# Attention and a two-layer feed-forward: weight signs carried by Prelu, inverse sums applied after the value product, q split by a difference

## The chip, the cores and the metric

The kernel runs on one core of one Trainium2 chip. The core's engines work side by side, each on its own instruction queue: TensorE (PE) multiplies matrices into PSUM; VectorE (DVE), ScalarE (ACT) and GpSimd (POOL) do elementwise work; SyncE (SP) issues DMAs. POOL does not read PSUM in this kernel. The metric is the time of one execution on the device in microseconds (us), lower is better.

## The reference

Eight batches of eight heads, 576 tokens, head dimension 64. Attention is causal by blocks of 64 tokens. Its output, heads side by side, is 4608 tokens of width 512 and goes through two layers with a leaky ReLU between them. q and k are about normal with a spread of 0.58, v of 0.1.

```
scores = q @ k.T / sqrt(64)
scores = where(pos_i // 64 >= pos_j // 64, scores, -1e9)
attn = exp(scores - max) ; attn = attn / (sum(attn) + 1e-9)
x = attn @ v                      # (4608, 512) after the heads are joined
h = x @ w_in                      # w_in (512, 2048), handed over in float64
out = maximum(0.01 * h, h) @ w_out  # w_out (2048, 512), float64
```

q, k and v are float32 and the weights are float64 in memory. The output is float32.

## The kernel before

**Precision and tiling.** A token row of scores needs up to 576 keys; each head has five query tiles (t = 0 to 4, the first of 64 tokens, the others of 128; tile t sees 64(2t+1) keys). Most products are made in pairs of 16-bit or rounded parts (a high part and the low part that is left), which keeps float32-like precision: q and k in `float32r` parts (`qs`, `kk`), v, x, the weights and the hidden layer in float16 parts. A matmul on full float32 data takes two PE records, and the trace shows each at about twice the time per column of a float32r or float16 one.

**Kinds of work.** Batch 0 is done as 8 `lo` items (tokens 0 to 319) and 8 `hi` items (320 to 575), with full float32 matmuls and no splitting (but for the scores of the `hi` items of heads 6 and 7, which are split as below): scores (L561), probabilities `p` in `prow` (the exponential, L609, whose row sums go to `sums`), inverse sums `rec` (L624 to L628, with a factor 2^15), `p` multiplied by `rec` in place (`normalising`, L676 to L678, on POOL, DVE or ACT), `p` transposed by PE (L724) and copied out of PSUM to `ptf` (`copying`, L259 and L260), value products into 64 rows of the PSUM bank `p_t` (L769), and a copy into `xr` (`put_x`, L748, through L259 or L260). Batch 1 is done as `first` items (tokens 0 to 191) and `rest` items (the others), batches 2 to 7 as whole heads (`full`, 48 of them). These split `p` into float16 parts (L653 to L658), transpose them by a DMA, and make value products with float16 operands (L784).

**The q and k split** (L521 to L534) of `first`, `rest` and `full`: q and k each stand twice, on partitions 0 to 63 and 64 to 127. `qs` gets 0.125 q rounded (L262 on ACT or L263 on DVE), then its lower half is replaced by the rest, 0.125 q minus the rounded part (L529, DVE only). `kk[:,0]` gets k rounded (L259 or L260), `kk[:,1]` the rest of k on all 128 partitions (L269 on DVE or L270 on POOL). One float32r matmul with each half of `kk` (L572) sums the high and low part of q over the 128 partitions.

**Weights.** Thirty-two pieces (16 of w_in, 16 of w_out), each 128 x 512 values of 8 bytes. A load goes to one of three buffers `raw` (L407). A piece takes four steps: the upper 32-bit word, read as float32, is scaled by 2^-112 (L411 ACT, L412 POOL or L413 DVE); the byte below the upper word gives further mantissa bits (L415, ACT); the sign bit of the upper word is merged into that (L416, DVE); the scaled word is shifted left by 3 bits, which drops its own sign, and joined with the result (L420, DVE). Then PE takes a Gram matmul of the piece (L434) for the size of the weights; after a layer's last piece follow the common scale and the split of all 16 pieces into float16 parts (L467 to L472).

**Feed-forward.** Eighteen chunks of 256 tokens: x is scaled and split (L905 to L909), the first layer (L925) writes `p_h`, ACT applies the leaky ReLU as Prelu (L930), a cast and a difference make the parts `gh` and `gl` (L259 or L260, L269 or L270) in a ring of 8, and the second layer (L943) sums in `p_o`.

**What sets the order.** Every instruction is handed to `Plan` with its candidate engines, an estimated cost, a rank, and what it reads and writes. `Plan.run` places them by a list schedule: an engine takes the ready operation with the lowest rank, and a second candidate is offered `HOLD` ns later than the first. The result is the fixed order of each engine's queue. Ranks count heads (batch 0's items count 1 each) and come from the constants at the top: `OFF1`, `SL1`, `AHEAD` and `OFF2` place the weight pieces, their loads and their splits, `RL` and `VD` the loads of q, k and v, `RP`, `RB`, `RN`, `RT`, `RV` and `RX` the steps of a head, `LEAD`, `LAG`, `RS` and `RG` the feed-forward. While PE would stand idle early on, the plan puts in a filler matmul of the identity (L1009), whose result is not used; it keeps PE at work.

Of the kernel before, what the change touches and what calls it, by code (L numbers as in the profile page):

```python
# [9 lines left out]
F32 = mybir.dt.float32  # L10
# [27 lines left out]
RW = -0.059  # L38

RL = 2.33  # L40
RP = 0.343
RB = 0.475
RT = 2.736
RV = 2.331
RX = -3.93
RN = -0.627

LEAD = 3.395
LAG = 1.993
RS = 2.118  # L50
RG = -0.005
OFF1 = 2.95
OFF2 = -5.023
SL1 = 10.227
AHEAD = 0.756

LAT = 1550
HOLD = 236.003
# [4 lines left out]
LOAD = 108  # L63
RATE = 0.4414
# [10 lines left out]
STEPA = 0.555  # L75
STEPB = 0.884
VD = 2.806
# [165 lines left out]
def attention_ffn(ctx: ExitStack, tc: tile.TileContext, qk0: bass.AP, qk: bass.AP, v: bass.AP, w_in: bass.AP, w_out: bass.AP, out: bass.AP):  # L243
# [13 lines left out]
    def copying(n, dst, src, sb=True, by=None, first="ACT", fast=True):  # L257
        if by is None:
            one = lambda: nc.scalar.copy(dst(), src())  # L259
            two = lambda: nc.vector.tensor_copy(dst(), src())  # L260
        else:
            one = lambda: nc.scalar.activation(dst(), src(), AF.Copy, scale=by)  # L262
            two = lambda: nc.vector.tensor_scalar_mul(dst(), src(), by)  # L263
        both = [("ACT", act(n, sb), one), ("DVE+" if sb and fast else "DVE", dve(n, sb and fast), two)]
# [18 lines left out]
    make_identity(nc, ident)  # L283
    ones = fixed([P, P], F32, "ones")
# [25 lines left out]
    for y in range(2):  # L310
        nc.gpsimd.memset(sums[y], 1.0)
# [65 lines left out]
    def weight_piece(num, rank, f, out_side):  # L377
# [26 lines left out]
        if src.dtype != F32:  # L404

            def load():
# [3 lines left out]
            add([  # L410
                ("ACT", act(w, True) + 70, lambda: nc.scalar.activation(val(), top(), AF.Copy, scale=2.0**-112)),  # L411
                ("POOL", pool1(w), lambda: nc.gpsimd.tensor_scalar(val(), top(), 2.0**-112, 1.0, op0=ALU.mult, op1=ALU.mult)),  # L412
                ("DVE+", dve(w), lambda: nc.vector.tensor_scalar_mul(val(), top(), 2.0**-112)),  # L413
            ], rank, [t_key], [v_key])
            add([("ACT", act(w, True) + 70, lambda: nc.scalar.activation(word(0), byte(), AF.Copy, bias=-15.5 / 32, scale=1 / 32))], rank, [], [r_key])  # L415
            add([("DVE+", dve(w) + 45, lambda: nc.vector.scalar_tensor_tensor(  # L416
                word(0), word(1), -2147483648, word(0), op0=ALU.bitwise_and, op1=ALU.bitwise_or
            ))], rank, [t_key], [r_key])
# [57 lines left out]
    def attention(i):  # L476
# [7 lines left out]
        plain_s, plain_v = kind == "lo" or kind == "hi" and h < HS, kind in ("lo", "hi")  # L484
# [39 lines left out]
        else:  # L524
            qd, khd, kld = qs[z][:, qa:qe], kk[z][:, 0, :ke], kk[z][:, 1, :ke]
            add(copying(qe - qa, lambda: qd, lambda: q_in, by=scale), rp, [qkey], [("qs", z)])
            add(copying(ke, lambda: khd, lambda: k_in), rp, [qkey], [("kh", z)])
            add(
                [("DVE+", dve(qe - qa) + 120, lambda: nc.vector.scalar_tensor_tensor(  # L529
# [517 lines left out]
```

## Time and profile before

| | |
|---|---|
| median of 3 runs | 1092.83 us (1090.83 to 1092.85) |
| the profiled execution | 1092.42 us |
| its span, first to last instruction | 1090.6 us |
| mean granted TensorE clock | 0.994 |
| busy: PE, DVE, ACT, POOL | 1047.4, 696.3, 671.3, 373.8 us |

A row of a group reads: line, engine, operation, out<-in by the program's names, out<-in as partitions x elements and type, xcount, then busy us and mean ns of one, then the engine's idle time before them and what ended it. A row of a stretch of the span gives each engine's busy us with its instruction count, then the granted clock, the DMA share and GB/s. A row in order of time gives start, duration, engine, line and operation. A row of waits gives who waited, for whom, the total in us, how many times, and the longest. PEld is PE's loading of the stationary operand, which overlaps PE.

### The profile page before, as it was taken

How to read it: one execution, taken by the hardware profiler on the slowest of the kernel's cores; microseconds unless marked ns; L12 is line 12 of the kernel's file. 1: busy time of each engine (PE TensorE's matmuls, PEld its weight loads, DVE VectorE, ACT ScalarE, POOL GpSimd, SP SyncE). 2: the span in 40 equal slices, each digit the busy share in tenths (PEclk: the TensorE clock that was granted, in tenths of full speed). 3: DMA queues.
4: the chain of work that ended last, by engine and by line, in shares of the span. 5: the costliest groups of instructions: out<-in, count | busy, mean ns of one | idle time of the engine just before them, and what ended most of it. 6: DMA issues, size and time to landing. Idle time of an engine off the chain costs nothing. (4 is left out here: it accounts for less than half of the span.)

```text
span 1090.6 us, 21865 instructions
## 1 busy us (share of the span) xinstructions
PE 1047.4 (96%) x8282; PEld 761.6 (70%) x8282; DVE 696.3 (64%) x1698; ACT 671.3 (62%) x1611; POOL 373.8 (34%) x423
## 2 busy tenths in 40 slices
PE   9999889999998889999999999999999999999998
PEld 7877557677665666677777777777777777766665
DVE  6797867888887787875655667777777775100000
ACT  5788846877787677655655575666666655322222
POOL 1112224445555443433323334333334342211221
PEclk9999999999999899999999999999999999999999
DMA  7837334798978577847355355757575654000000
GB/s 272 269 124 237 91 90 113 149 214 177 183 152 183 103 162 146 177 99 158 82 125 104 88 128 116 157 112 153 121 155 121 125 82 95 1 20 11 10 20 20
DMA packets 251017, 134.85 MB, mean 124 GB/s; under 512 B 221728, under 2 KB 232992, under 8 KB 250912
## 3 DMA queue, kind: packets, MB, share of 16 engines
q1 hardware_dynamic: 250912, 133.46, 53.0%
q8 instruction: 65, 1.06, 0.4%
q14 instruction: 40, 0.33, 0.1%
HBM read 68.94 MB, written 9.44 MB: 72 GB/s over the span
## 5 line engine op out<-in xcount | busy, mean ns | idle before, releaser
L925 PEld LDWEIGHTS <-wih 128*128 128x128 f16 x2304 | 222.3, 99 | 72.2 <-issue 3.2
L270 POOL TENSOR_TENSOR gl<-g,gh 128x512 bf16<-128x512 f32 x115 | 136.5, 1188 | 284.3 <-ACT gh L259 246.0
L925 PE MATMUL p_h<-slab,wih 128*128 128x256 f16 x1152 | 197.9, 274 | 3.2 <-DVE xi L896 2.2
L930 ACT ACTIVATE g<-p_h 128x512 f32<-128x512 f32 x144 | 85.0, 591 | 154.5 <-PE p_h L925 149.5
L943 PE MATMUL p_o<-woh,gh 128*128 128x512 f16 x576 | 172.2, 381 | 0.0
L943 PE MATMUL p_o<-woh,gl 128*128 128x512 f16 x576 | 172.1, 380 | 0.0
L943 PE MATMUL p_o<-wol,gh 128*128 128x512 f16 x576 | 171.9, 380 | 0.0
L943 PEld LDWEIGHTS <-gh 128*128 128x128 f16 x1152 | 107.2, 99 | 80.7 <-issue 1.3
L592 DVE TENSOR_REDUCE nm<-p_s 128x1 f32<-128x320 f32 (+4 forms) x308 | 140.8, 488 | 31.6 <-ACT prow L609 15.1
L925 PE MATMUL p_h<-xh,wih 128*128 128x256 f16 x576 | 158.2, 275 | 0.3 <-ACT g L930 0.3
L925 PE MATMUL p_h<-xl,wih 128*128 128x256 f16 x576 | 158.0, 274 | 0.0
L925 PE MATMUL p_h<-xh,wil 128*128 128x256 f16 x576 | 157.9, 274 | 0.0
L925 PE MATMUL p_h<-slab,wil 128*128 128x256 f16 x576 | 157.8, 274 | 0.0
L572 PE MATMUL p_s<-kk,qs 128*128 128x288 f32 (+3 forms) x592 | 124.3, 334 | 24.6 <-ACT slab L609 15.2
L609 ACT ACTIVATE prow<-p_s,nm 128x448 f32<-128x448 f32 (+4 forms) x168 | 88.4, 530 | 75.7 <-DVE nm L592 71.1
L925 PEld LDWEIGHTS <-wil 128*128 128x128 f16 x1152 | 113.4, 98 | 14.9 <-issue 1.2
L572 PEld LDWEIGHTS p_s<-kk,qs 128*128 128x128 f32 x592 | 90.9, 190 | 45.5 <-ACT slab L609 22.8
L609 ACT ACTIVATE slab<-p_s,nm 128x320 f32<-128x320 f32 (+4 forms) x140 | 72.5, 522 | 63.4 <-DVE nm L592 62.6
L270 POOL TENSOR_TENSOR kk<-qk_in,kk 128x576 fp32r<-128x576 f32 (+1 forms) x51 | 75.6, 1483 | 89.2 <-ACT kk L259 34.4
L943 PEld LDWEIGHTS <-gl 128*128 128x128 bf16 x576 | 56.5, 98 | 68.4 <-issue 0.8
L658 DVE SCALAR_TENSOR_TENSOR slab<-prow,rec,slab 128x320 f16<-128x320 f32 (+4 forms) x140 | 85.9, 648 | 22.5 <-ACT slab L654 20.1
L784 PEld LDWEIGHTS <-vs 128*128 128x128 f16 x1680 | 85.9, 98 | 11.1 <-issue 2.5
(135 smaller groups left out, 1524.0 us busy)
## 6 DMA issues: line engine op xcount, KB each, us to landing
qk_in<-in_qk SPq DMA_DIRECT2D x56, 576.0 KB, 4.3
raw<-in_w_in SPq DMA_DIRECT2D x16, 512.0 KB, 4.7
raw<-in_w_out SPq DMA_DIRECT2D x16, 512.0 KB, 4.5
out<-ob SPq DMA_DIRECT2D x18, 256.0 KB, 2.4
out<-slab SPq DMA_DIRECT2D x18, 256.0 KB, 3.1
v_raw<-in_v SPq DMA_DIRECT2D x7, 640.0 KB, 6.2
raw<-in_v SPq DMA_DIRECT2D x7, 640.0 KB, 5.7
qk_in<-in_qk SPq DMA_DIRECT2D x8, 416.0 KB, 3.7
```

The costliest lines, as they stand in the source:

```text
L270: ("POOL", pool2(n) - (0.25 * n if n == 512 else 0), lambda: nc.gpsimd.tensor_sub(dst(), one(), two())),
L572: go = lambda ap=ap, cols=cols, c=c, k0=k0, k1=k1, first=first, last=last: nc.tensor.matmul(ap, qs[z][:, cols], kk[z][:, c, k0:k1], start= ...
L592: [("DVE", dve(kw[t]), lambda t=t, ap=ap, flat=flat: nc.vector.tensor_reduce(nm[z][: qn[t], t : t + 1], ap[: qn[t]], axis=AX.X if flat els ...
L609: nc.scalar.activation(o, ap[: qn[t]], AF.Exp, bias=nm[z][: qn[t], t : t + 1], scale=scale / 2 if plain_s else 1.0, accum_out=sums[z][: qn ...
L658: ("DVE+", dve(w) + 62, lambda: nc.vector.scalar_tensor_tensor(part(1), p, by, part(0), op0=ALU.mult, op1=ALU.subtract)),
L784: nc.tensor.matmul(p_t[x][:, c : c + src.free_size()], vs[z][:, (j + 1) % NT], src, start=start, stop=stop)
L925: nc.tensor.matmul(hh[:, i, :], w[:, f, d, :], x[:, d, :], start=k == 0, stop=k == len(terms) - 1)
L930: add([("ACT", act(512), lambda: nc.scalar.activation(g[z], hh, AF.Prelu, alpha=0.01, scale=DOWN))], rank, [("h", z)], [("g", z)])
L943: nc.tensor.matmul(p_o[m], a[:, i, m * P : (m + 1) * P], w[:, 2 * u + i, :], start=u == 0 and k == 0, stop=u == NU - 1 and k == 5,)
```

## The change

Five things change.

- **Weight pieces.** The upper word is scaled by a Prelu on ACT with slope 2^32 for negative values, so a negative value's exponent is 32 higher. After the left shift by 3, this exponent bit is the sign bit. The merge of the sign (L416) is gone, and so are the POOL and DVE forms of the scaling (L412, L413).
- **Batch 0.** `normalising` is gone; `p` stays unnormalised. A float32 matmul per tile of `rec`, spread over 64 columns, with the identity puts the inverse sums of all tokens on 64 partitions of the other PSUM bank (`spread`). The copy into `xr` now copies these, and a DVE multiplication by the value product follows, in place.
- **The q and k split.** Both copies take a factor per partition from a new constant `eighth`: q is scaled by 0.125 on partitions 0 to 63 and by 1 on the others, k the other way round. q's low part is then a plain difference on 64 partitions, on DVE or POOL; k's low part is only made on partitions 0 to 63, with zeros on the others from the start. The copy's ACT form is planned with 93 ns more.
- **`first` items** take the full float32 scores of batch 0 (`plain_s`), with no split of q and k.
- **Constants.** The ranks and engine offers are refitted, and the plan now knows a longer load (`LOADS`, 190 ns) for the score matmuls, 108 before.

```
-RL = 2.33
+RL = 4.147
-RP = 0.343
+RP = -0.26
-RT = 2.736
+RT = 3.569
-RX = -3.93
+RX = -5.745
-RN = -0.627
+RN = -1.226
-LEAD = 3.395
+LEAD = 3.858
-OFF1 = 2.95
-OFF2 = -5.023
-SL1 = 10.227
-AHEAD = 0.756
+OFF1 = 3.4
+OFF2 = -3.708
+SL1 = 12.623
+AHEAD = -3.272
-STEPB = 0.884
-VD = 2.806
+STEPB = 0.691
+VD = 1.444
...
+    eighth = fixed([P, 2], F32, "eighth")
+    nc.gpsimd.memset(eighth, 1.0)
+    nc.gpsimd.memset(eighth[0:64, 0:1], scale)
+    nc.gpsimd.memset(eighth[64:128, 1:2], scale)
...
+        nc.gpsimd.memset(kk[y][64:128, 1].bitcast(F32), 0.0)
...
-            add([
-                ("ACT", act(w, True) + 70, lambda: nc.scalar.activation(val(), top(), AF.Copy, scale=2.0**-112)),
-                ("POOL", pool1(w), lambda: nc.gpsimd.tensor_scalar(val(), top(), 2.0**-112, 1.0, op0=ALU.mult, op1=ALU.mult)),
-                ("DVE+", dve(w), lambda: nc.vector.tensor_scalar_mul(val(), top(), 2.0**-112)),
-            ], rank, [t_key], [v_key])
+            add([("ACT", act(w, True) + 70, lambda: nc.scalar.activation(val(), top(), AF.Prelu, alpha=2.0**32, scale=2.0**-112))], rank, [t_key], [v_key])
...
-            add([("DVE+", dve(w) + 45, lambda: nc.vector.scalar_tensor_tensor(
-                word(0), word(1), -2147483648, word(0), op0=ALU.bitwise_and, op1=ALU.bitwise_or
-            ))], rank, [t_key], [r_key])
...
-        plain_s, plain_v = kind == "lo" or kind == "hi" and h < HS, kind in ("lo", "hi")
+        plain_s, plain_v = kind == "lo" or kind == "hi" and h < HS or kind == "first", kind in ("lo", "hi")
...
+            add(copying(qe - qa, lambda: qd, lambda: q_in, by=eighth[:, 0:1]), rp, [qkey], [("qs", z)])
+            add(copying(ke, lambda: khd, lambda: k_in, by=eighth[:, 1:2]), rp, [qkey], [("kh", z)])
+            add(subtracting(qe - qa, lambda: qd[64:128], lambda: q_in[64:128], lambda: qd[64:128]), rp, [qkey], [("qs", z)])
+            add(subtracting(ke, lambda: kld[0:64], lambda: k_in[0:64], lambda: khd[0:64]), rp, [qkey, ("kh", z)], [("kl", z)])
...
-                else:
-                    add(normalising(t, qn[t]), r0 - RN, [("rec", z, t)], pkeys(t))
...
+                add(copying(n, dst, lambda: p_t[x0][0:64, :n], sb=False), rx, [("t", x0)], keys)
+                add([("DVE", dve(n) + 100, lambda: nc.vector.tensor_mul(dst(), p_t[x][0:64, :n], dst()))], rx, [("t", x)], keys)
...
+            def spread(t):
+                n, c = qn[t], q0[t] - tokens[kind][0]
+                return 4 * RATE * n, lambda: nc.tensor.matmul(
+                    p_t[x0][0:64, c : c + n], rec[z][:n, t : t + 1].to_broadcast([n, 64]), ident[:n, :n], start=True, stop=True
+                )
+
+            mine = {"lo": (0, 1, 2), "hi": (3, 4)}[kind]
+            add([("PE", [spread(t) for t in mine])], rv, [("rec", z, t) for t in mine], [("t", x0)])
```

More of the change, by code (lines that the diff above doesn't have):

```diff
@@ L37 @@
 AHEADV = 3
-RW = -0.059
-RL = 2.33
-RP = 0.343
-RB = 0.475
-RT = 2.736
-RV = 2.331
-RX = -3.93
-RN = -0.627
-LEAD = 3.395
-LAG = 1.993
-RS = 2.118
-RG = -0.005
-OFF1 = 2.95
-OFF2 = -5.023
-SL1 = 10.227
-AHEAD = 0.756
+RW = -0.109
+RL = 4.147
+RP = -0.26
+RB = 0.357
+RT = 3.569
+RV = 2.503
+RX = -5.745
+RN = -1.226
+LEAD = 3.858
+LAG = 1.993
+RS = 2.261
+RG = 0.075
+OFF1 = 3.4
+OFF2 = -3.708
+SL1 = 12.623
+AHEAD = -3.272
 LAT = 1550
-HOLD = 236.003
+HOLD = 238.351
 FILL = 235
@@ L63 @@
 LOAD = 108
+LOADS = 190
 RATE = 0.4414
@@ L74 @@
 SIDE = 34
-STEPA = 0.555
-STEPB = 0.884
-VD = 2.806
+STEPA = 0.564
+STEPB = 0.691
+VD = 1.444
 JOINT = 0
@@ L261, in copying @@
         else:
-            one = lambda: nc.scalar.activation(dst(), src(), AF.Copy, scale=by)
+            one = lambda: nc.scalar.mul(dst(), src(), by)
             two = lambda: nc.vector.tensor_scalar_mul(dst(), src(), by)
-        both = [("ACT", act(n, sb), one), ("DVE+" if sb and fast else "DVE", dve(n, sb and fast), two)]
+        both = [("ACT", act(n, sb) + (93 if by is not None else 0), one), ("DVE+" if sb and fast else "DVE", dve(n, sb and fast), two)]
         return both if first == "ACT" else both[::-1]
@@ L667, in turning @@
             add([("SP", TISSUE, turn)], r0 - RN, [("ph", y2, alias[t], y) for t in ts for y in (0, 1)], [("pt", y2, alias[t]) for t in ts], lag=TMOVE * (e - a))
-        def normalising(t, rr):
-            by = rec[z][:rr, t : t + 1]
-            def p():
-                return row(t, rr, pc[t], kw[t])
-            return [
-                ("POOL", pool1(kw[t]), lambda: nc.gpsimd.tensor_scalar(p(), p(), by, 1.0, op0=ALU.mult, op1=ALU.mult)),
-                ("DVE+", dve(kw[t], True), lambda: nc.vector.tensor_scalar_mul(p(), p(), by)),
-                ("ACT", act(kw[t], True), lambda: nc.scalar.mul(p(), p(), by)),
-            ]
         ready_ = []
@@ L747, in put_x @@
             if plain_v:
-                add(copying(n, dst, lambda: p_t[x][0:64, c : c + n], sb=False), rx, [("t", x)], keys)
+                add(copying(n, dst, lambda: p_t[x0][0:64, :n], sb=False), rx, [("t", x0)], keys)
+                add([("DVE", dve(n) + 100, lambda: nc.vector.tensor_mul(dst(), p_t[x][0:64, :n], dst()))], rx, [("t", x)], keys)
                 return
@@ L759, in put_x @@
             )
-        x0 = bank() if kind == "full" else None
+        x0 = bank() if kind == "full" or plain_v else None
         x1 = bank()
@@ L773, in attention @@
             values = [product(p_t[x1][:, c : c + e - a], j, slice(a, e), j == 1, j == last) for j, a, e, c in spans[kind]]
+            def spread(t):
[5 more added lines that the diff above has]
+            add([("PE", [spread(t) for t in mine])], rv, [("rec", z, t) for t in mine], [("t", x0)])
             if kind in ends:
                 c, w = ends[kind]
-                add([("PE", [product(p_t[x0][:, :w], 0, slice(c, c + w), True, True)])], rv, ptd + [vkey], [("t", x0)])
+                add([("PE", [product(p_t[x1][:, :w], 0, slice(c, c + w), True, True)])], rv, ptd + [vkey], [("t", x1)])
             add([("PE", values)], rv, ptd + [vkey], [("t", x1)])
```

14 lines of the change are left out of this document (3 added, 11 removed).

## The prediction

> **What bounds the kernel now.** I read the page's engine totals first, then the busy time by stretches of the span.
>
> ```profile
> span 1090.6 us, 21865 instructions
> PE 1047.4 (96%) x8282; PEld 761.6 (70%) x8282; DVE 696.3 (64%) x1698; ACT 671.3 (62%) x1611; POOL 373.8 (34%) x423
> ```
>
> ```profile
> core 0: us, PE busy (x) PEld busy (x) DVE busy (x) ACT busy (x) POOL busy (x), PEclk, DMA share, GB/s
> 0.00:120.00 120.00, 111.94 (x841) 92.01 (x842) 95.25 (x238) 93.26 (x225) 21.91 (x44) 1.00 0.67 222
> 60.00:80.00 20.00, 18.69 (x161) 16.19 (x159) 19.39 (x32) 17.09 (x33) 4.36 (x3) 1.00 0.28 84
> ...
> 180.00:510.00 330.00, 307.48 (x2573) 225.39 (x2572) 265.39 (x633) 245.18 (x604) 154.02 (x168) 0.98 0.75 157
> 510.00:930.00 420.00, 416.02 (x3427) 302.76 (x3426) 283.11 (x687) 253.84 (x617) 145.89 (x165) 1.00 0.55 117
> ```
>
> From 510 us on, PE has 4 us idle in 420 and nothing on another engine can gain there. Between 180 and 510 it idles 22.5 us in 330. The first 120 us look just as full (111.94), but the same stretch for the filler matmul of L1009 alone, whose result nobody reads, says otherwise:
>
> ```profile
> 0.00:120.00 120.00, 28.85 (x208) 26.11 (x208) 1.00 0.67 222
> ```
>
> So PE does no useful work for 28.85 + 8.06 = 36.9 of 120 us. That is the stage which reads the weights and does batch 0's attention; DVE and ACT are both near 78% busy in it. What ends it shows in the order of time:
>
> ```profile
> 114.77 0.69 DVE L420 SCALAR_TENSOR_TENSOR slab<-slab,raw 128x512 int32<-128x512 int32 x1
> ...
> 116.10 0.40 PE L434 MATMUL p_o<-slab 128*128 128x128 bf16 x4
> ...
> 118.01 4.40 ACT L467 ACTIVATE woh<-slab,ws 128x512 f16<-128x512 f32 x7 [0.30 <-DVE ws L370]
> ...
> 119.85 0.59 PE L943 MATMUL p_o<-woh,gh 128*128 128x512 f16 x2
> ```
>
> The last piece of w_out leaves DVE at 115.46, its Gram matmuls follow, then the common scale, the split, and at 119.85 the first second-layer matmul. From there PE has long work. The stage therefore ends when the 32 weight pieces are through DVE and ACT. The waits of the DMA queue in the first 120 us say what paces the pieces:
>
> ```profile
> SPq L407 <- DVE slab L420: 48.1, 22, 15.3
> ```
>
> The weight loads (L407) waited 48.1 us for a raw buffer, and each buffer is given back by the DVE instruction L420, last of its piece.
>
> **The change, part by part.** *The weight pieces.* These are the rows that go, and the row of the instruction that stays in another form (Prelu for Copy), with its 26 on ACT; the other six were POOL's.
>
> ```profile
> L416 DVE SCALAR_TENSOR_TENSOR raw<-raw 128x512 int32<-128x512 int32 x32 | 24.1, 760 | 3.4 <-ACT raw L415 3.3
> L411 ACT ACTIVATE slab<-raw 128x512 f32<-128x512 f32 x26 | 17.4, 670 | 9.0 <-DMA raw<-in_w_in 8.6 <-DMA raw<-in_w_out 0.4
> L677 DVE TENSOR_SCALAR prow<-prow,rec 128x192 f32<-128x192 f32 (+3 forms) x12 | 3.7, 345 | 0.0
> L678 ACT ACTIVATE prow<-prow,rec 64x64 f32<-64x64 f32 (+3 forms) x13 | 6.7, 525 | 2.9 <-DVE rec L628 2.8
> ```
>
> DVE loses 24.1 us of merges. ACT takes the six POOL pieces: 6 x 0.670 = +4.0 us. I give Prelu the Copy's price: the kernel's other Prelu (L930) is the nearest row, shown here with a copy of the same size out of PSUM, 591 against 580 ns, so 32 x 0.011 = 0.4 us at most.
>
> ```profile
> L930 ACT ACTIVATE g<-p_h 128x512 f32<-128x512 f32 x144 | 85.0, 591 | 154.5 <-PE p_h L925 149.5 <-PE p_t L784 4.6
> L259 ACT COPY ptf<-p_t 128x512 f32<-128x512 f32 x13 | 7.4, 580 | 6.1 <-PE p_t L724 6.0
> ```
>
> *Batch 0's normalising.* In the stage DVE loses 3.7 us and ACT 6.7 (rows above; POOL's share is not near a bound). Added are 16 products of a PSUM and an SBUF operand on DVE, 320 or 256 columns wide. No such row exists; the nearest is the DVE addition that also reads PSUM and the destination:
>
> ```profile
> L755 DVE SCALAR_TENSOR_TENSOR slab<-p_t,vin,slab 64x512 f32<-64x512 f32 x24 | 17.8, 741 | 4.5 <-ACT slab L751 4.1
> L755 DVE SCALAR_TENSOR_TENSOR slab<-p_t,vin,slab 64x192 f32<-64x192 f32 x8 | 3.3, 410 | 1.8 <-ACT slab L751 1.5
> ```
>
> That is (741 - 410)/320 = 1.03 ns a column, 0.54 us for 320 and 0.48 for 256, so 8 x 1.02 = +8.1 us. The copy into x stays, only its source changes. So ACT and DVE together, which had 95.25 + 93.26 = 188.5 us, lose 24.1 + 3.7 + 6.7 and gain 4.0 + 8.1: net -22.4, or 11.2 an engine if the order keeps them level, which it can: casts, copies and splits have a form for either.
>
> What of the 11.2 is on the path? Outside 60 to 80 us DVE is busy 95.25 - 19.39 = 75.9 of 100 us; the rest is waits that don't shrink. I take 11.2 x 0.76 = **8.5 us** off the stage's end. Bounds: nothing, if the loads or PE's waits set the pace; and 22 x 0.76 = 16.7 us, if each of the 22 waits of the load queue becomes one merge shorter.
>
> PE gets 40 fp32 matmuls that spread the inverse sums, two records each. By the fillers, of the same 128 columns,
>
> ```profile
> 50.15 2.05 PE L1009 MATMUL p_o<-ident 128*128 128x128 f32 x16
> ```
>
> a record takes 2.05/16 = 0.128 us, so 80 take 10.2 us. I cost them at nothing: they take the place of fillers (28.85 us) and idle time (8.06). With that cover gone they cost the 10.2. The spread waits for the reciprocal, as the normalising did, but the transposes no longer do. The added clears are on POOL, busy 21.91 of 120 us: nothing.
>
> *Batch 1's first part* has no conversions any more, in exchange for fp32 scores and one small scaling.
>
> ```profile
> L529 DVE SCALAR_TENSOR_TENSOR qs<-qk_in,qs 64x192 fp32r<-64x192 f32 x8 | 3.2, 395 | 0.4 <-ACT qs L262 0.2
> L262 ACT ACTIVATE qs<-qk_in 128x192 fp32r<-128x192 f32 x7 | 2.5, 359 | 4.0 <-PE p_s L572 2.7 <-DMA qk_in<-in_qk 1.3
> L601 DVE TENSOR_SCALAR nm<-nm 128x3 f32<-128x3 f32 (+1 forms) x15 | 2.3, 151 | 0.1
> L561 PE MATMUL p_s<-qk_in 128*128 128x192 f32 x8 | 2.3, 376 | 0.0
> L572 PE MATMUL p_s<-kk,qs 128*128 128x192 f32 x112 | 28.8, 266 | 1.4 <-ACT slab L609 1.4
> ```
>
> DVE and ACT lose 3.2 + 2.5 and gain 8 x 0.151 = 1.2: -4.5, half of it per engine, -2.2. PE gains (376 - 266) x 2 records x 8 = 1.8 us, and a third of that again for the 64 columns: +2.4. I take 0, with bounds -4.5 and +2.4.
>
> *The other heads.* q's low part becomes a plain difference that POOL may also take; both copies now read their factor per partition.
>
> ```profile
> L529 DVE SCALAR_TENSOR_TENSOR qs<-qk_in,qs 64x576 fp32r<-64x576 f32 x48 | 57.1, 1190 | 1.5
> L269 DVE TENSOR_TENSOR kk<-qk_in,kk 128x576 fp32r<-128x576 f32 x12 | 9.2, 764 | 0.2
> L270 POOL TENSOR_TENSOR kk<-qk_in,kk 128x576 fp32r<-128x576 f32 x46 | 72.5, 1576 | 80.2 <-ACT kk L259 31.2 <-DVE kk L260 25.5 <-DVE rec L625 12.6
> L262 ACT ACTIVATE qs<-qk_in 128x576 fp32r<-128x576 f32 x46 | 31.2, 678 | 5.6 <-PE p_s L572 5.3
> L259 ACT CAST kk<-qk_in 128x576 fp32r<-128x576 f32 x34 | 22.4, 659 | 0.0
> L467 ACT ACTIVATE woh<-slab,ws 128x512 f16<-128x512 f32 x16 | 9.9, 707 | 0.3 <-DVE ws L370 0.3
> L259 ACT CAST gh<-g 128x512 f16<-128x512 f32 x134 | 82.2, 614 | 2.5
> ```
>
> On DVE a difference costs 764 ns where the old form took 1190: 48 x 0.426 = -20.4 us. The factor per partition costs ACT 707 - 614 = 93 ns on 46 + 34 copies: +7.4. Net -13, of which the 22 heads or so before 510 us have 6; PE idles there only 22.5 of 330 us, so 6/2 x 0.07 = 0.2. I take 0; bounds -6 and +3.4 (7.4 x 22/48, all of it on PE's path).
>
> The sum, against the profiled execution (1092.42 us; its span is 1090.6; the median of the three runs, 1092.83, is 0.4 above): 1092.42 - 8.5 + 0 + 0 = **1083.9**.
>
> *A rule against it.* L529's 576 columns take 1190 ns where 192 take 395; at the slope of the 1.03 ns above, 576 would take 0.79, so 0.4 us of each is a stall, on average; POOL works at the neighbouring difference for 1576 ns meanwhile. The Trainium skill (GPSIMD Engine Reference, Specifications) says that POOL's way into SBUF is shared with VectorE and collides with DVE instructions that have two SBUF inputs; the trace agrees by that 0.4 us. By the rule, a second difference on POOL doubles the time in which DVE is held: its result is the third rival below.
>
> **The rivals.** *The weights come last.* The refit moves the last piece's rank from 2.95 + 10.227 = 13.18 to 3.4 + 12.623 = 16.02, and a rank is a head, 119.85/16 = 7.5 us: the pieces fall back 2.84 x 7.5 = 21.3 us in the order, behind all heads of batch 0. Place: the first L943. With 8.5 us of work less it would come at 119.85 + 21.3 - 8.5 = 132.6; PE would have heads and first-layer work meanwhile, but with the present 36.9/120 = 31% of the time lost, 0.31 x 12.8 = 4 us more are lost: 1096.4. It decides for slower once L943 starts later than now. For it: nothing but that matmul ends the stage. Against: DVE and ACT have idle time that weights fill whatever their rank.
>
> *The stage is paced elsewhere.* The DMA share is 0.67 in it, and DVE's idle time is spent waiting for PE's scores. Then the freed time becomes idle time: 1092. Against it stands the 48.1 us wait for L420.
>
> *POOL holds DVE.* Should POOL take q's difference in the 22 heads before 510 us, DVE is held another 22 x 0.4 = 8.8 us there; if all of it reaches PE, the 8.5 are eaten: 1092.7.
>
> *All of it is on the path*, and more: 16.7 us off the stage, 1075.7; and two stretches run below full clock,
>
> ```profile
> 150.00:170.00 20.00, 16.75 (x114) 12.27 (x113) 14.29 (x47) 11.09 (x36) 5.64 (x3) 0.91 0.38 105
> 340.00:370.00 30.00, 23.62 (x196) 17.74 (x195) 23.36 (x58) 21.14 (x49) 13.96 (x14) 0.83 0.65 141
> ```
>
> which cost 20 x 0.09 + 30 x 0.17 = 6.9 us; an order without PE's pauses there gains these too, one with more pauses loses as much.
>
> **How the numbers follow.** Forecast (1079 to 1090) 0.42; all on the path 0.16; paced elsewhere 0.12; POOL holds DVE 0.06; weights last 0.16; more pauses of PE in the new order 0.08, up to 1099. About 0.2% (2.2 us) is what a measurement of this kernel tells from no change. Faster: 0.42 + 0.16 and 0.02 of POOL's case, 0.60; same: 0.12 + 0.04, 0.16; slower 0.24. The range takes in the full gain with a part of the clock's 6.9 us below, and the late weights with 3 us for the copies above: 1073 to 1099; the forecast's own is 1079 to 1090.
>
> **What would show it.** First L943 near 111 us, fillers down by about 10 us or more, the load queue's wait for L420 well below 48.1, ACT about as busy as before up to there and DVE less: right. Wrong: L943 at 120 or later; the spread on PE after the fillers have ended, pushing scores; q's differences on POOL with long DVE rows beside them; a gain that lies between 180 and 510 us, which would be the new order's and not the removed work's.

## The result and the profile after

The changed kernel took 1110.22 us (median of 5 runs, 1109.35 to 1111.41); the kernel before, on the same chip, 1090.83 (1089.90 to 1092.85). The ratio is 1.0174 with a 95% interval of 1.0158 to 1.0189: slower by 19 us where 8.5 us less were forecast, and beyond the range's upper end of 1099. The differences below are ratios to runs of the kernel before on the same chip; where one is given in us, it is the ratio less 1, times 1091. Times of single rows, and spans, are of the profiled executions.

The engine totals of the changed kernel, and its busy time by stretches (the same columns as in the prediction):

```profile
span 1107.6 us, 21815 instructions
PE 1057.2 (95%) x8300; PEld 767.1 (69%) x8300; DVE 677.1 (61%) x1677; ACT 677.7 (61%) x1580; POOL 387.7 (35%) x400
```

```profile
0.00:120.00 120.00, 115.95 (x864) 93.40 (x865) 83.07 (x221) 94.33 (x218) 16.98 (x35) 1.00 0.68 224
120.00:240.00 120.00, 115.76 (x875) 81.81 (x874) 86.20 (x227) 82.13 (x204) 51.38 (x54) 1.00 0.57 129
240.00:360.00 120.00, 102.34 (x841) 74.48 (x839) 99.20 (x220) 83.60 (x206) 55.66 (x59) 0.94 0.71 154
360.00:510.00 150.00, 135.58 (x1110) 99.80 (x1111) 119.35 (x294) 109.05 (x262) 68.72 (x68) 0.95 0.66 146
510.00:930.00 420.00, 413.76 (x3385) 300.04 (x3382) 276.59 (x695) 257.79 (x613) 159.09 (x155) 1.00 0.54 116
```

The same stretches of the kernel before, from 120 us on:

```profile
120.00:240.00 120.00, 112.95 (x836) 78.32 (x834) 94.45 (x247) 85.02 (x215) 47.97 (x52) 0.99 0.56 127
240.00:360.00 120.00, 108.17 (x908) 78.56 (x908) 100.61 (x239) 91.87 (x233) 64.05 (x70) 0.97 0.80 170
360.00:510.00 150.00, 141.44 (x1183) 104.22 (x1182) 113.91 (x276) 104.18 (x255) 61.83 (x67) 0.99 0.70 141
```

Up to 120 us things went roughly as forecast. DVE has 12.2 us less (95.25 to 83.07; 11.2 were forecast), ACT stays level (93.26 to 94.33). Up to 240 us PE is even fuller than before, but not with more useful work: without fillers and spread (shown below) it is 82.5 us in the first 120, before 83.1. The loss lies from 240 to 510 us: PE idles 32.1 us there (17.7 + 14.4) where it idled 20.4, and its clock falls to 0.94 and 0.95 where it was 0.97 and 0.99. From 510 to 930 us it idles 6.2 us, before 4.0.

The next fence groups instructions of the changed kernel by line and shape (busy us and mean ns of one; idle us before them). Then, from the stretches of one line each, the fillers (L999, first fence) and the spread (L758, second fence); and last the DMA queue's largest wait in the first 120 us.

```profile
L416 ACT ACTIVATE slab<-raw 128x512 f32<-128x512 f32 x32 | 21.4, 668 | 6.4 <-DMA raw<-in_w_in 5.9 <-DMA raw<-in_w_out 0.2
L730 DVE TENSOR_TENSOR xr<-p_t,xr 64x320 f32<-64x320 f32 x8 | 3.9, 484 | 3.1 <-PE p_t L751 1.4 <-ACT raw L417 1.0 <-ACT slab L416 0.5
L730 DVE TENSOR_TENSOR xr<-p_t,xr 64x256 f32<-64x256 f32 x8 | 3.3, 415 | 2.1 <-PE p_t L751 1.8
L263 ACT ACTIVATE kk<-qk_in,eighth 128x576 fp32r<-128x576 f32 x55 | 41.9, 762 | 0.1
L270 DVE TENSOR_TENSOR qs<-qk_in,qs 64x576 fp32r<-64x576 f32 x21 | 20.5, 974 | 0.7
L271 POOL TENSOR_TENSOR qs<-qk_in,qs 64x576 fp32r<-64x576 f32 x27 | 40.8, 1512 | 25.8 <-issue 11.0 <-DVE slab L651 3.9 <-DVE p_s L583 2.6
```

```profile
0.00:120.00 120.00, 22.34 (x146) 19.39 (x146) 1.00 0.68 224
```

```profile
0.00:120.00 120.00, 11.14 (x72) 7.22 (x72) 1.00 0.68 224
120.00:180.00 60.00, 1.30 (x8) 0.82 (x8) 1.00 0.36 87
```

```profile
SPq L413 <- DVE slab L419: 29.7, 16, 11.1
```

The fillers fell by 6.5 us and the spread took 12.4. The weight loads wait 29.7 us for a buffer where they waited 48.1. The last Gram matmuls (L433), and the first second-layer matmul (L933) with what stands right before it in PE's queue:

```profile
108.41 0.39 PE L433 MATMUL p_o<-slab 128*128 128x128 bf16 x4
...
114.22 0.65 PE L758 MATMUL p_t<-ident,rec 128*64 128x128 f32 x4
114.71 1.90 PE L751 MATMUL p_t<-ptf,vf 128*64 128x256 f32 x10
116.54 0.61 PE L933 MATMUL p_o<-woh,gh 128*128 128x512 f16 x2
```

The stage ends at 116.54 instead of 119.85: 3.3 us of the 8.5, although the last Gram matmuls come 7.7 us sooner (116.10 to 108.41). Behind them PE's queue holds other work, the last of it a spread and a value product.

### The profile page after: what moved, and what is told of

Its sections match the earlier page's. It is cut to its first block, busy times and chain, and to the rows that moved or that the text cites. A ratio compares the mean times of both kernels' runs of the same rounds, so it can differ in the third digit from the quotient of the medians.

```text
span 1107.6 us, 21815 instructions
## 1 busy us (share of the span) xinstructions
PE 1057.2 (95%) x8300; PEld 767.1 (69%) x8300; DVE 677.1 (61%) x1677; ACT 677.7 (61%) x1580; POOL 387.7 (35%) x400
## 5 line engine op out<-in xcount | busy, mean ns | idle before, releaser
L271 POOL TENSOR_TENSOR gl<-g,gh 128x512 bf16<-128x512 f32 x109 | 128.4, 1178 | 329.5 <-ACT gh L260 219.1
L933 PE MATMUL p_o<-woh,gh 128*128 128x512 f16 x576 | 173.8, 384 | 0.0
L933 PE MATMUL p_o<-wol,gh 128*128 128x512 f16 x576 | 173.2, 383 | 0.0
L933 PE MATMUL p_o<-woh,gl 128*128 128x512 f16 x576 | 172.7, 382 | 0.0
L587 DVE TENSOR_REDUCE nm<-p_s 128x1 f32<-128x320 f32 (+4 forms) x308 | 143.5, 490 | 39.9 <-ACT slab L604 18.0
L933 PEld LDWEIGHTS <-gh 128*128 128x128 f16 x1152 | 107.6, 99 | 83.2 <-issue 3.3
L567 PE MATMUL p_s<-kk,qs 128*128 128x288 f32 (+3 forms) x560 | 122.0, 343 | 38.5 <-ACT prow L604 17.5
L567 PEld LDWEIGHTS p_s<-kk,qs 128*128 128x128 f32 x560 | 88.6, 194 | 64.4 <-ACT slab L604 26.5
L915 PEld LDWEIGHTS <-wil 128*128 128x128 f16 x1152 | 113.0, 98 | 13.7 <-issue 0.3
L933 PEld LDWEIGHTS <-gl 128*128 128x128 bf16 x576 | 56.8, 99 | 69.2 <-issue 2.2
L651 DVE SCALAR_TENSOR_TENSOR slab<-prow,rec,slab 128x320 f16<-128x320 f32 (+4 forms) x140 | 85.6, 633 | 15.9 <-ACT slab L647 13.6
L651 DVE SCALAR_TENSOR_TENSOR slab<-slab,rec 128x320 f16<-128x320 f32 (+4 forms) x140 | 83.8, 624 | 16.8 <-ACT slab L647 14.5
L774 PE MATMUL p_t<-slab,vs 128*128 128x128 f16 (+1 forms) x1680 | 90.8, 212 | 2.2 <-DMA slab<-slab 1.9
```

What stands on the lines that cost most here:

```text
L271: ("POOL", pool2(n) - (0.25 * n if n == 512 else 0), lambda: nc.gpsimd.tensor_sub(dst(), one(), two())),
L567: go = lambda ap=ap, cols=cols, c=c, k0=k0, k1=k1, first=first, last=last: nc.tensor.matmul(ap, qs[z][:, cols], kk[z][:, c, k0:k1], start= ...
L587: [("DVE", dve(kw[t]), lambda t=t, ap=ap, flat=flat: nc.vector.tensor_reduce(nm[z][: qn[t], t : t + 1], ap[: qn[t]], axis=AX.X if flat els ...
L651: ("DVE+", dve(w) + 62, lambda: nc.vector.scalar_tensor_tensor(part(1), p, by, part(0), op0=ALU.mult, op1=ALU.subtract)),
L774: nc.tensor.matmul(p_t[x][:, c : c + src.free_size()], vs[z][:, (j + 1) % NT], src, start=start, stop=stop)
L915: nc.tensor.matmul(hh[:, i, :], w[:, f, d, :], x[:, d, :], start=k == 0, stop=k == len(terms) - 1)
```

## The experiments

| kernel | order | ratio to before, 95% |
|---|---|---|
| the changed kernel | its own | 1.0174 (1.0158 to 1.0189) |
| q_diff_on_dve | the changed kernel's | 1.0219 (1.0194 to 1.0244) |
| q_diff_dve_planned | planned anew | 1.0261 (1.0234 to 1.0287) |
| q_split_old_order | before's | 1.0015 (1.0005 to 1.0024) |
| prelu_old_order | before's | 0.9984 (0.9975 to 0.9994) |
| prelu_planned | planned anew | 1.0011 (1.0002 to 1.0020) |
| prelu_fewer_fillers | before's | 0.9972 (0.9959 to 0.9985) |
| first_plain_old_order | before's | 0.9975 (0.9965 to 0.9984) |
| first_plain_planned | planned anew | 1.0031 (1.0020 to 1.0043) |
| order_nudged_rp | planned anew | 0.9987 (0.9977 to 0.9998) |
| before_new_constants | planned anew | 1.0101 (1.0086 to 1.0116) |
| after_old_constants | planned anew | 1.0138 (1.0118 to 1.0157) |
| spread_planned | planned anew | 1.0176 (1.0156 to 1.0196) |
| spread_old_order | before's | 1.0125 (1.0110 to 1.0140) |
| spread_fewer_fillers | before's | 1.0107 (1.0090 to 1.0125) |
| after_spread_left_out | the changed kernel's | 1.0109 (1.0081 to 1.0137) |
| after_normalised | planned anew | 1.0149 (1.0126 to 1.0172) |
| after_normalised_old_constants | planned anew | 0.9961 (0.9948 to 0.9974) |
| after_ffn_later | planned anew | 1.0172 (1.0148 to 1.0196) |

### Does POOL hold DVE?

**q_diff_on_dve**: the changed kernel's order, each q difference issued on DVE.

```
-  add(subtracting(qe - qa, ...), rp, [qkey], [("qs", z)])
+  diff = subtracting(qe - qa, ...)
+  add([diff[0], (*diff[1][:2], diff[0][2])], rp, [qkey], [("qs", z)])
```

> The changed kernel in its own planned order; only where the plan put q's low part (the 64 x 576 difference) on POOL, the same instruction is issued to DVE at that place. Three theories for the 19 us lost between 210 and 510 us. POOL holds DVE (the difference on POOL stalls DVE instructions with two SBUF inputs): 1094 to 1101, and the rows of rec and of L651 above 1.2 us disappear from 240 to 330 us. The refitted order (ranks that fit the chip worse, whatever engine makes the difference): within 3 us of the changed kernel's 1110. Dearer copies with a factor per partition on ACT: within 3 us of 1110.

**q_diff_dve_planned**: POOL isn't offered the q difference, and the order is planned anew (`subtracting(...)[:1]`).

> The changed kernel with q's difference offered to DVE alone, so that the whole order is planned anew. POOL holds DVE: 1088 to 1100. The refitted order: 1103 to 1113. Dearer copies: 1105 to 1112. Against the run that only moves the instruction it also shows what planning anew does by itself.

**q_split_old_order**: the kernel before in its own order, with the new copies (factor per partition), the plain q difference on DVE and k's difference on 64 partitions.

```
-  add(copying(qe - qa, lambda: qd, lambda: q_in, by=scale), ...)
+  add(copying(qe - qa, lambda: qd, lambda: q_in, by=eighth[:, 0:1]), ...)
-      qd[64:128], q_in[64:128], scale, qd[64:128], op0=ALU.mult, op1=ALU.subtract
+      nc.vector.tensor_sub(qd[64:128], q_in[64:128], qd[64:128])
```

> The kernel before in its own planned order; in place, the two copies take their factor per partition, q's low part is the plain difference on DVE (where the other form stood), k's low part is made on 64 partitions. Theory of the order: 1087 to 1093. Theory of dearer instructions (the copies with a factor per partition, 93 ns each on ACT, delay the exponentials): 1095 to 1103.

The stall is real. In the order of time of the changed kernel, a DVE instruction of 2 columns lasts until two POOL differences, of k and of `gl`, are through (rows of other engines left out):

```profile
298.85 1.41 POOL L271 TENSOR_TENSOR kk<-qk_in,kk 64x576 fp32r<-64x576 f32 x1
...
299.18 2.22 DVE L620 TENSOR_SCALAR rec<-sums 128x2 f32<-128x2 f32 x1 [1.19 <-ACT slab L604]
...
300.23 1.15 POOL L271 TENSOR_TENSOR gl<-g,gh 128x512 bf16<-128x512 f32 x1
```

Neither of the two is q's difference, which POOL had done just before. But that difference adds to such stalls: the 26 instructions of this shape take 558 ns on average in the changed kernel and 216 with q's differences on DVE. A stall can also reach PE. From 259.64 to 265.40 us POOL was at work almost without a break, q's difference first, and two instructions of L651 (564 ns each on average) took 4.63 us; the exponential that waits for DVE's next maximum (L587) came late:

```profile
261.12 4.63 DVE L651 SCALAR_TENSOR_TENSOR slab<-prow,rec,slab 128x192 f16<-128x192 f32 x2
...
267.60 0.63 ACT L604 ACTIVATE slab<-p_s,nm 128x448 f32<-128x448 f32 x1 [3.59 <-DVE nm L587]
```

PE then waited 3.58 us, until 269.57, its longest wait between 240 and 390 us.

Yet POOL's hold isn't the loss: with the difference on DVE that wait is gone, but PE's waits for the exponential in these 150 us grow from 13.6 to 21.9 us, and the kernel became 4.9 us slower in the same order (1.0219 less 1.0174), 9.5 us planned anew. Not all of the 4.9 need be the difference's. In the profiled execution 4.5 us were lost by the first first-layer matmul (68.5 against 64.0 us), while the first q difference of either kernel comes after 100 us. Its first 20 us, then those of the changed kernel:

```profile
0.00:20.00 20.00, 15.66 (x78) 13.14 (x79) 5.93 (x19) 7.71 (x22) 3.29 (x24) 0.83 0.70 245
```

```profile
0.00:20.00 20.00, 17.14 (x108) 14.30 (x108) 8.39 (x30) 10.11 (x28) 3.29 (x24) 1.00 0.88 293
```

So taking the difference off POOL gained nothing; how much it cost stays open. The split by itself costs 1.6 us in the old order.

### The weights

**prelu_old_order**: the kernel before in its own order; the Prelu wherever the scaling stood, the merge left out.

```
-  nc.scalar.activation(val(), top(), AF.Copy, scale=2.0**-112)      # and its POOL and DVE forms
+  nc.scalar.activation(val(), top(), AF.Prelu, alpha=2.0**32, scale=2.0**-112)
-  add([("DVE+", dve(w) + 45, lambda: nc.vector.scalar_tensor_tensor(word(0), word(1), ...))], ...)
+  add([("DVE+", dve(w) + 45, lambda: None)], ...)
```

> The kernel before in its own planned order; in place, the weight scaling is the Prelu on ACT (also where the plan has it on POOL) and the merge is left out, its place in DVE's queue empty. Nothing else changes. Theory of the order (what was lost came from a planned order that fits the chip worse, since any change of instructions plans everything anew): 1081 to 1087, the early stage's gain goes through to the end. Theory of the middle's pace (210 to 510 us is limited by attention's chains, an earlier start there is lost again): 1088 to 1092.

**prelu_planned**: the same part of the change as the changed kernel has it, before's constants, planned anew.

> The kernel before, its constants kept, with the weight pieces alone as in the changed kernel and everything planned anew. Theory of the order: 1088 to 1105, at least 5 us slower than the same instructions in the old order. Theory of the middle's pace: like the same instructions in the old order, within 3 us.

**prelu_fewer_fillers**: prelu_old_order with two of each five fillers left out.

```
   def fill():
+      count[0] += 1
+      if count[0] % 5 not in (1, 3):
           nc.tensor.matmul(p_o[1][:, 0:P], ident, ident, start=True, stop=True)
```

> As prelu_old_order (order of before, Prelu in place, the merges left out; it took 1089.3), with two of each five filler matmuls left out. Theory 'the fillers hold back what the weights part gains': up to 11 us less, 1078 to 1086. Rival 'the chain of the weight pieces sets the stage's end and the fillers only stand in its waits': 1087 to 1091. Rival 'PE's clock falls with its load': 1092 or more, with a granted clock below 0.98 in the first 120 us.

The part gains 1.7 us in the old order, 3.1 with fewer fillers, and planned anew it loses 1.2. Its work did go: in prelu_planned the first second-layer matmul starts at 112.1, as forecast (111), against 119.85. It doesn't reach the end. Of the fillers, 10.2 us taken out (28.85 to 18.62) gave 1.3 us, with overlapping intervals. PE waits in their place, for the softmax and the first layer's activations, and the third theory's sign was there too, a clock below 0.98, though the time it named was not:

```profile
0.00:120.00 120.00, 107.57 (x767) 84.57 (x768) 76.99 (x210) 97.29 (x234) 17.10 (x38) 0.97 0.67 222
```

A clock of 0.97 over 120 us is up to 3.6 us (1.00 with all fillers), which may have taken back a part of the gain.

### The plain scores

**first_plain_planned**: the one change `or kind == "first"` in `plain_s`, before's constants.

> The kernel before with one part alone: the scores of batch 1's first part are plain fp32 products of q and k, without conversions. Constants as before; planned anew. Theory 'this part slows the heads' (its fp32 records hold PE while batch 1's first heads wait): 1097 or more, with the last value product of batch 1 later than 263.7 us. Rival 'its work is too small to matter' (8 heads by at most 0.3 us of PE): 1088 to 1094.

**first_plain_old_order**: fp32 scores in the places of the split ones, the conversions left out. A load may overwrite q and k there before the scores have read them (it stands where the conversions had released them), so batch 1's values need not be the reference's.

> The kernel before, same order of instructions: batch 1's first part has plain fp32 scores, its conversions are left out where they stood. Theory 'the order, not the work': 1089 to 1093, the 4.5 us of removed DVE and ACT work not seen. Rival 'fp32 scores hold PE among the heads': 1094 or more.

Small: -2.7 us in place (the forecast's bound was -4.5) and +3.4 planned anew.

### Constants, and whether before's order is a lucky one

**before_new_constants** and **after_old_constants** exchange the 19 planner constants of the diff between the two kernels (LOADS at 108, the planner's common value, with the old ones). **order_nudged_rp** is the kernel before with `RP = 0.4` for 0.343.

> The kernel before with the refitted constants (all but LOADS, which it has no use for); no instruction is changed. The refitted order: 1103 to 1115, the loss between 210 and 510 us is there without any changed instruction. POOL holds DVE, or dearer copies: 1088 to 1096.

> The changed kernel with all refitted constants (ranks, offers, LOADS) set back to the values of before; every changed instruction stays. POOL holds DVE: still slow, 1103 to 1112, if the plan gives as many differences to POOL. The refitted order: 1083 to 1092, since the early stage's gain of some 7 us stays and the middle recovers. Dearer copies: 1103 to 1112.

> The kernel before with one constant nudged, RP 0.343 to 0.4: the same instructions, another order (some of them on another engine). Theory of the order: 1094 to 1106, a nudge costs as much as the changes did, because the old order is a picked one. Otherwise: 1089 to 1093.

Another order of the same instructions can be just as fast (-1.4 us), so before's is no single lucky one. The new constants make the kernel before 11 us slower, but the changed kernel with the old ones is still 15 us slower than before: something in the changed work is dear too.

### The spread

**spread_planned**: before with batch 0's part of the change alone (normalising out; spread, its bank and the DVE product in), before's constants.

> The kernel before with one part of the change alone: batch 0's p isn't normalised, its value product is multiplied by spread inverse sums. Constants as before; the order is planned anew. With before's constants the whole change costs 14 us, the weights alone 1, the q split (in before's order) 2. Theory 'the seam': batches 1 and 2 pace PE up to about 350 to 365 us, so what counts is when the fifth chunk of the first layer starts and how much time there is from it to the end. If the spread is what delays the heads of batches 1 and 2 (its p_t bank is taken from the kind of product that they use too, and batch 0's second part lies among batch 1's heads), the fifth chunk starts at 370 us or later and the time is 1100 or more. Rival 'q's difference, planned, is the cause': within 3 us of 1091.

**spread_old_order**: before's order, the spread directly behind the last value product, the DVE product behind the copy, the normalising left out where it stood.

```
-  ("DVE+", dve(kw[t], True), lambda: nc.vector.tensor_scalar_mul(p(), p(), by)),    # and its POOL and ACT forms
+  ("DVE+", dve(kw[t], True), lambda: None),
+  values[-1] = (values[-1][0], behind(values[-1][1]))    # spread(t) for the item's tiles
+  nc.vector.tensor_mul(dst(), p_t[x][0:64, :n], dst())   # behind copying(... p_t[1 - x] ...)
```

> The kernel before, same order of instructions: batch 0's normalising is left out where it stood, the spread follows the last value product on PE into the other p_t bank, and the DVE product stands directly behind the copy into x. That bank can still hold values that have not been read, so batch 0's values need not come out as the reference's; the work is that of the change. Theory 'the order, not the work, makes the loss': 1085 to 1093. Rival 'the work of the spread itself, 80 records and 16 DVE products, slows the heads': 1096 or more.

**spread_fewer_fillers**: the same with two of each five fillers left out.

> As spread_old_order (same order as before, spread behind the last value product; batch 0's values need not be the reference's), with two of each five filler matmuls left out, about 84 of 208 records or 11.7 us. Theory 'the spread has no cover, for the fillers stand in PE's queue by number and don't shrink': with fewer of them it is covered, 1092 to 1096. Rival 'the spread delays batch 0's chain through the p_t bank, the copy and the product on DVE': 1101 or more, PE idle in the first 75 us in their place.

**after_spread_left_out**: the changed kernel's order, with `lambda: None` for the spread matmul and for the DVE product.

> The changed kernel in its own order with the 40 spread matmuls and the 16 DVE products left out, so batch 0's values are not scaled as the reference's are. Theory 'the records' own time': PE has 12 us less in the first 150 us, and the time falls by 8 to 12 us, to 1098 to 1102. Rival 'the seam': the heads of batches 1 and 2 set when the fifth chunk starts (367.8 us now), and the time stays within 4 us of 1110.

The spread alone costs 19.2 us planned anew and 13.6 in the old order. PE's busy time in the first 120 us, with all fillers and with fewer (spread_old_order, then spread_fewer_fillers):

```profile
0.00:120.00 120.00, 112.99 (x854) 91.82 (x854) 89.33 (x209) 80.30 (x195) 15.13 (x32) 1.00 0.63 207
```

```profile
0.00:120.00 120.00, 105.99 (x783) 83.13 (x783) 92.07 (x216) 83.03 (x202) 15.80 (x32) 1.00 0.62 210
```

Fewer fillers took 7 us of work off PE and only 2.0 us off the time (1.0125 to 1.0107, intervals overlapping): PE idles in their place. So it isn't only that PE is full; batch 0's chain from item to item got longer. From the first to the last of the eight value products of `lo` items it is 34.8 us before (14.25 to 49.02), 43.8 in spread_old_order (13.46 to 57.24) and still 42.1 with fewer fillers (12.90 to 54.99). The sixth and the seventh of them, in the order of time: before, then spread_fewer_fillers:

```profile
40.88 1.20 PE L769 MATMUL p_t<-ptf,vf 128*64 128x64 f32 x8
...
44.46 1.20 PE L769 MATMUL p_t<-ptf,vf 128*64 128x64 f32 x8
```

```profile
44.06 1.20 PE L778 MATMUL p_t<-ptf,vf 128*64 128x64 f32 x8
...
45.20 0.90 PE L791 MATMUL p_t<-ident,rec 64*64 64x64 f32 x6
...
47.08 0.48 DVE L260 COPY xr<-p_t 64x320 f32<-64x320 f32 x1 [0.47 <-PE p_t L724]
...
47.59 0.48 DVE L753 TENSOR_TENSOR xr<-p_t,xr 64x320 f32<-64x320 f32 x1
...
48.13 0.33 PE L724 MATMUL p_t<-ident,prow 128*128 128x128 f32 x1 [0.59 <-DVE xr L753]
...
48.86 1.20 PE L778 MATMUL p_t<-ptf,vf 128*64 128x64 f32 x8
```

Before, one item follows the other by 3.6 us. Here it is 4.8, with PE waiting 0.59: value product, spread (0.9), transposes, copy into x, product on DVE, and only then may the last transpose write its `p_t` bank (it waits for L753), after which come the copy into `ptf` and the next value product. The DVE product stands in this chain, as the spread does. PE's waits for it in the first 120 us are

```profile
PE p_t L724 <- DVE xr L753: 2.2, 3, 0.8
```

so the chain is shown, but how much of the loss is its and how much the records' own time is not. In the old order the delay is 8.5 us at the first first-layer matmul (64.9 to 73.4), and from the second chunk on (157.1 to 169.6) everything stands 12 to 14 us later to the end.

The changed kernel has another chain. Its plan puts an item's spread in front of the value product, and in the first 180 us PE waits for no product on DVE (L730). In this order the spread and the product account for 7.1 us (1.0174 less 1.0109), between what the two theories named: 8 to 12 and at most 4.

Planned anew under before's constants, most of the loss comes later than batch 0's stage. In spread_planned the first second-layer matmul starts at 124.33 us, 4.5 later than before, and the fifth chunk of the first layer at 384.8, 25.3 later; the span ends 20.2 us later. Why the heads in between are so much later is not shown.

### Put together

**after_normalised**: the changed kernel with `normalising` as before and no spread, new constants. **after_normalised_old_constants**: the same with before's constants (LOADS 108).

```
+  else:
+      add(normalising(t, qn[t]), r0 - RN, [("rec", z, t)], pkeys(t))
-  add([("PE", [spread(t) for t in mine])], rv, [("rec", z, t) for t in mine], [("t", x0)])
-  add([("DVE", dve(n) + 100, lambda: nc.vector.tensor_mul(dst(), p_t[x][0:64, :n], dst()))], rx, ...)
```

> The changed kernel with batch 0's p normalised as before, and without the spread matmuls, their bank and the DVE products; Prelu, the q split, the plain scores and all new constants stay, and the order is planned anew. Theory 'the spread is the whole loss': 1087 to 1094 (the changed kernel less some 19 us). Rival 'the new constants or the q split slow the heads between 240 and 390 us by themselves' (the kernel before with the new constants took 1101.6): 1100 or more.

> The changed kernel without the spread (p normalised as before) and with the constants of before: Prelu, q split and plain scores, planned anew. With the spread and these constants it took 1104.8, with the new constants and without the spread 1107.2. Theory 'two losses that don't add: the spread, and an order that no longer fits': 1088 to 1096 here, so the spread alone takes some 10 us under the old constants, and the new ones bring nothing without it. Rival 'the q split, planned, slows the heads under any constants': 1101 or more.

**after_ffn_later**: the changed kernel with `LEAD = 4.458` for 3.858.

> The changed kernel with one constant changed: LEAD 4.458 for 3.858, so every chunk of the two layers stands 0.6 head later in the order, behind the heads. Theory 'early PE time went to the two layers, which run out before the fifth chunk can start': the heads get that time, their first 480 value matmuls (changed kernel: 165 to 375 us, before: 171 to 364) end at 371 or sooner, the fifth chunk's first matmul comes before 365, and the time is 1104 or less. Rival 'the heads go at their own pace through DVE and ACT, whatever PE does between them': 480th value matmul within 2 us of 375, time 1108 or more (later layers leave more for the end).

The four kernels with Prelu, q split and plain scores, in us against before:

| | p normalised | spread |
|---|---|---|
| old constants | -4.3 (-5.7 to -2.8) | +15.1 (+12.9 to +17.1) |
| new constants | +16.3 (+13.7 to +18.8) | +19.0 (+17.2 to +20.6) |

Under the old constants the spread costs 19.3 us. The new constants cost 20.5 us without it and 3.9 with it. The two losses don't add, and it is symmetric: on top of the new constants the spread costs 2.7 us, with overlapping intervals. Taking away one of the two alone brings back 2.7 or 3.9 us, both together 23.2. The rest of the change is worth 4.3 us, and that kernel is faster than both. Its second layer starts when the forecast said:

```profile
112.37 0.59 PE L938 MATMUL p_o<-woh,gh 128*128 128x512 f16 x2
```

The theory that PE gave its early time to the two layers instead of to the heads, and that a later place for the layers would mend it, fell: after_ffn_later is as slow as the changed kernel (1.0172). Its rows, then those of after_normalised, then of after_normalised_old_constants:

```profile
240.00:360.00 120.00, 101.35 (x838) 74.56 (x837) 95.84 (x235) 85.48 (x216) 54.43 (x59) 0.93 0.79 166
360.00:510.00 150.00, 134.53 (x1109) 100.48 (x1108) 120.77 (x289) 108.74 (x267) 67.20 (x66) 0.94 0.67 146
```

```profile
240.00:360.00 120.00, 100.91 (x846) 74.43 (x844) 97.17 (x239) 86.48 (x217) 51.28 (x54) 0.94 0.77 164
360.00:510.00 150.00, 137.34 (x1148) 102.99 (x1149) 121.00 (x291) 105.69 (x259) 68.07 (x68) 0.97 0.67 140
```

```profile
240.00:360.00 120.00, 102.67 (x863) 75.87 (x861) 96.30 (x231) 88.82 (x221) 60.86 (x67) 0.96 0.75 167
360.00:510.00 150.00, 142.31 (x1185) 105.40 (x1185) 117.70 (x280) 102.82 (x252) 66.81 (x70) 0.98 0.69 141
```

All three idle some 17 to 19 us on PE between 240 and 360 us, the fast one too, which had come ahead by then and lost that lead. From 360 to 510 us the two with new constants idle another 15.5 and 12.7 us, the fast one 7.7 (before 8.6).

The waits of PE between 240 and 390 us show what it waits for: scores, held up by the softmax. The changed kernel, then the kernel before:

```profile
PE p_s L567 <- ACT slab L604: 8.4, 6, 3.2
PE p_s L567 <- ACT prow L604: 5.2, 4, 2.6
PE p_s L567 <- DVE slab L651: 3.6, 1, 3.6
PE p_s L567 <- POOL v_raw L537: 2.6, 1, 2.6
```

```profile
PE p_s L572 <- ACT slab L609: 8.8, 7, 3.0
PE p_s L572 <- ACT prow L609: 4.2, 6, 2.1
```

The waits for the exponential are about the same (13.6 and 13.0 us). What the changed kernel has more of is single waits, of 3.6 us behind the stall of L651 and of 2.6 us.

Counted from the matmul records, the two layers have used up everything at hand by 360 us: before and after have then both done four chunks (768 of the first layer's matmuls, 384 of the second's), and the fifth starts once the heads allow it, at 359.5 before, 367.8 after, 358.9 with the spread left out, 360.7 in after_normalised_old_constants, 369.8 in after_normalised. At 240 us the changed kernel was ahead by 16,896 matmul columns of the two layers (about 7 us, at 0.11 us from start to start of a 256-column matmul) and level in the heads' score and value columns; that lead is worth nothing at 360 us. But the fifth chunk's start doesn't settle the end. Of the 17.0 us between the two profiled spans 8.3 are there at that start and 8.7 come behind it; with the spread left out it comes 0.6 us sooner than before, and the span still ends 8.0 us later (1098.6). Which constants slow the heads, and how, stays open.

## Why the prediction was wrong

**Two steps failed. The first is batch 0's normalising**: "I cost them at nothing: they take the place of fillers (28.85 us) and idle time (8.06)." The spread cost 13.6 us in the old order, 19.2 and 19.3 planned under the old constants, against 0 and a bound of 10.2. Four things were wrong in it. The fillers are instructions that the planner writes into PE's queue by its own estimates, not time that gives way: the spread kernels keep 208 and 210 of them (208 before), and only the spread and the new constants together bring them to 146. Of the spread's 80 records 28 start after the changed kernel's last filler (75.2 us), so they had none to replace. The records took 12.4 us where 10.2 was worked out (0.156 each against 0.128). And the spread and the DVE product were counted as engine time, but in before's order they stand in the chain from one item of batch 0 to the next, which stayed 7.3 us longer over the eight `lo` items when fillers were taken out. That the spread costs this under before's constants is shown by exchange; the mechanism of the planned kernels, where most of the loss comes behind batch 0, stays open.

**The second is a term that was missing**: the order that the new constants make. The prediction took the constants up only by the weights' rank and by pauses of PE worth up to 6.9 us. They cost 20.5 us without the spread, 11 us in the kernel before, and 3.9 with the spread. As the spread costs 2.7 under them, neither is by itself the cause of the 19 us; each alone is enough for 15 to 16. The rival nearest to what happened was "more PE pauses in the new order", given 0.08 and 1099 at most: PE does idle more from 240 to 510 us, at a lower clock, but its size was too small.

**Weights first**, right up to the stage's end, wrong beyond it. DVE's 12.2 us and ACT's level are as worked out; Prelu costs what Copy did (668 against 670 ns); the loads' wait fell from 48.1 to 29.7. Without the spread, and with before's constants, the second layer starts at 112.37 (forecast 111). But of those 7.5 us only 4.3 reach the end, with q split and plain scores in it, and of prelu_planned's 7.7 none. The step "the stage's end is 8.5 us earlier, so is the end" fails in these planned orders by about 360 us, where the two layers have run out of chunks and the heads set the pace: the fifth chunk of prelu_planned starts at 362.0, before at 359.5.

**The other durations** were good: the DVE products took 484 and 415 ns (forecast 540 and 480), the factor per partition 762 ns against 659 (+103; forecast +93). q's difference on DVE took 974 ns, not 764. In place, the q split cost 1.6 us and the plain scores gained 2.7, inside their bounds; planned anew the plain scores cost 3.4, beyond theirs (+2.4).

**The rivals.** "The weights come last" would decide with the first second-layer matmul later than 119.85: in the changed kernel it came at 116.54, so no; but the new constants alone did that to the kernel before (128.5). "POOL holds DVE" showed its stalls, one of which reached PE, but moving the difference off POOL gained nothing. On the rule of the Trainium skill (GPSIMD Engine Reference, Specifications), the trace agrees that DVE instructions with two SBUF inputs are held beside POOL, with 4.63 us for two of L651; the instruction of 2 columns that took 2.22 us reads one tensor only. What the rule cannot say is what the kernel gains or loses by using POOL here. "Paced elsewhere" was nearest to what became of the early gain, only that the place is the heads up to 360 us and behind, and not the first stage.

## What to carry to other kernels

Work put on an engine "in the place of idle time" is free only if what fills that time gives way, and if the new work isn't in the chain that causes the idling: follow one item of the loop, bank by bank, before counting engine time. A stage that ends earlier is worth what the next stage that runs out of work lets through; look for the point where the long work is used up and something else starts it again. Planner constants are part of a change: price them by exchanging them alone, with and without the new code. Where two losses don't add, neither run alone tells the cause; all four combinations do.

## What the runs showed of the hardware

PE's pauses can cost twice, by their own time and by the clock. The changed kernel's stretches around two of its long waits, PE's busy time and clock:

```profile
265.00:275.00 10.00, 6.42 (x22) 0.73 0.56 113
275.00:285.00 10.00, 9.73 (x91) 0.93 0.59 164
...
360.00:370.00 10.00, 6.75 (x30) 0.58 0.71 157
```

Around a pause of 3.58 us (the wait for L651 above, until 269.57) the granted clock was 0.73 over 10 us and 0.93 over the next, together 3.4 us of clock, nearly the pause's own length. The Trainium skill (TensorE: Matmul & The Clock Gate, HAM oscillation) warns of gaps of PE above some 3.4 us. That pause agrees with it, but shorter ones did the same here: from 360 us on the clock was 0.58, and PE's longest wait there was the 2.6 us for L537; in the first 20 us of q_diff_on_dve it was 0.83, with no wait above 2.17. Between 240 and 510 us the mean clocks of the rows come to 14.7 us below full speed in the changed kernel (120 x 0.06 + 150 x 0.05) and 5.1 before (120 x 0.03 + 150 x 0.01). These 9.6 us more are at most what the clock cost, as clock that is withheld while PE idles costs nothing; the added idle time is 11.7 us.

In a fixed order a delay passes through unchanged: the 12.5 us that spread_old_order lost by 157 us are 13.3 at its end. Planned anew, parts worth 1 to 3 us in place came out 1 to 3 us on the other side.
